# Holding the request of the fifth q and k until V of batch 1 has landed, in an attention and maxout-MLP kernel

## The chip, the cores and the metric

One core of a Trainium2 chip. The metric is device time in microseconds (us), the median of several executions. "Span" is the time from the first to the last instruction in the profile; the device time is 1.7 to 1.8 us more. Every execution reports the mean clock that TensorE was granted (1.000 is full), but only one of each set leaves a trace, so a trace always belongs to one execution with its own time. A run that is over 1.5% above the fastest of its kernel counts as slow; ratios leave such runs out, medians here keep them. A "hole" is a stretch in which TensorE stands idle, and the "flight" of a transfer is its time from request to landing.

## The reference

```python
# q, k, v: (8 batches, 8 heads, 576, 64)
attn = softmax(mask(q @ k.T / sqrt(64)))      # causal by blocks of 64
x = (attn @ v) as (4608 tokens, 512)
out = maximum(x @ w1, x @ w2) @ w_out         # w1, w2: (512, 1024), w_out: (1024, 512)
```

## The kernel before

The kernel runs attention for pairs of heads and fills TensorE's gaps with matmuls of the MLP. The 16 loads of q and of k ("groups" 0 to 15, two per batch) come through three buffers. A group's way is: transfer as float32, a Pool cast to bf16, TensorE transposes, copies, score matmuls.

```python
    def load_qk(g, queues, gated=False):
        ...
            raws[nm, g] = t = raw.tile([P, 2, RPP * D], FP32, name=f"{nm}raw")
            if gated:
                nc.gpsimd.memset(t[:, 0, :1], 0.0)     # one column: the transfer waits for Pool's turn
            queue.dma_start(out=t[:], in_=...)
```

A "gated" load can be requested only when Pool has come to its memset (the fifth q's starts at 38.41 us in the trace, the request follows at 38.55). Around the change, in program order (cuts marked):

```python
    load_qk(3, (SP, SP), gated=True)         # fourth q and k
    for c in range(NCH):
        load_v(1, c)                         # V of batch 1: five chunks, from Pool's DMA queue
    ...
    cast("q", 3, ((pool, 0, RPP),))
    cast("k", 3, ((pool, 0, RPP),))
    ...
    transposes("q", 3, (dve, act))()
    pool_work(4)                             # requests the fifth q and k (group 4)
    fill(n // 3)
    transposes("k", 3, (dve, act))()
    pad_keys(6)
    pad_keys(7)
    pool_work(5)                             # requests group 5, casts group 4
    ...
    for g in range(GPB + 1, NG):             # first turn, g = 3:
        ...
            av_with(p - LAG, lo)             # matmuls that read V of batch 1
            ...
            copy_out = t_pair(p)             # transposes of the fifth q
```

The whole kernel:

The softmax here doesn't subtract the row's maximum and nothing guards it: scores larger than these inputs give would overflow.

## Time and profile before

| | before |
|---|---|
| median of the first three runs | 259.31 us (259.14 to 260.01) |
| the run whose trace was read | 260.0 us, span 258.2 us |
| TensorE busy | 247.4 us, 96% |
| hole of TensorE before the fifth q's transposes, in that trace | 1.61 us |
| fifth q, request to landing | 38.55 to 46.06 us |
| last chunk of V of batch 1 lands | 44.87 us |

The lines are in the prediction. "PE" is TensorE, and an arrow in brackets names what ended an idle stretch.

### The profile page before, as it was taken

To read this page: it belongs to the slowest core of one execution; us is meant where nothing else is said; L and a number is where in the kernel's file an instruction comes from. 1 tells how busy PE (TensorE), PEld (TensorE's weight loads), DVE (VectorE), ACT (ScalarE), POOL (GpSimd) and SP (SyncE) were. 2 spreads that over 40 slices of the span, in tenths; PEclk is the share of its full clock that TensorE was granted. 3 is DMA by queue.
4 is the path that set the end of the run, shared out by engine and by line. 5 is a ranking of instruction groups with operands and counts; after the bars stand their busy time and mean duration, and the time that the engine had idled before them with its cause. 6 is when DMAs were issued, how large, how long until landed. Compare 5 with 4: busy or idle time off the path is not lost.

```text
span 258.2 us, 7195 instructions
## 1 busy us (share of the span) xinstructions
PE 247.4 (96%) x2983; PEld 139.1 (54%) x2983; DVE 136.1 (53%) x299; ACT 143.2 (55%) x200; POOL 110.4 (43%) x274
## 2 busy tenths in 40 slices
PE   7598899799999999999999999999999999999995
PEld 2346678646555555555555554546464655444444
DVE  4967986556584428451845184518550853443200
ACT  2798854476574857586757665766576431000111
POOL 1987950584637263726382638163813010000000
PEclk9999999999999999999999999999999999999999
DMA  6999999499569995998599949985977122202122
GB/s 244 316 206 307 217 251 246 156 102 253 129 162 257 144 188 135 245 154 225 114 244 143 186 145 224 168 196 141 91 109 110 44 56 80 83 0 81 43 104 99
DMA packets 71265, 41.30 MB, mean 160 GB/s; under 512 B 53568, under 2 KB 58048, under 8 KB 71232
## 3 DMA queue, kind: packets, MB, share of 16 engines
q1 hardware_dynamic: 28544, 31.27, 43.4%
q0 software_dynamic: 42272, 8.92, 39.9%
q10 hardware_dynamic: 416, 0.66, 0.7%
q8 instruction: 23, 0.38, 0.6%
q14 instruction: 10, 0.08, 0.1%
HBM read 34.60 MB, written 9.44 MB: 171 GB/s over the span
## 4 chain that ended last, share of the span: by engine, by line
PE 84%; DMA 8%; POOL 3%; ACT 2%; issue 1%; DVE 0%; SPq 0%; POOLq 0%; ACTq 0%
PE ps_y L257 36%; PE ps_h L215 22%; PE ps_o L479 10%; PE ps_s L371 8%; DMA qraw<-in_q_dram 5%; DMA kraw<-in_k_dram 3%; PE ps_qT L352 2%; PE ps_kT L352 2%; PE ps_w L341 1%; ACT aT L395 1%; PE ps_y L272 1%; PE ps_M L238 1%; POOL kn L132 1%; PE ps_s L389 1%; ACT qT L360 1%
## 5 line engine op out<-in xcount | busy, mean ns | idle before, releaser
L395 ACT ACTIVATE aT<-ps_s 128x1024 bf16<-128x1024 f32 (+2 forms) x100 | 95.8, 996 | 25.8 <-PE ps_s L371 24.2
L257 PE MATMUL ps_y<-wo_sb,g 128*128 128x512 bf16 x280 | 69.8, 379 | 0.0
L215 PE MATMUL ps_h<-xT,d_sb 128*128 128x512 bf16 (+3 forms) x320 | 69.2, 358 | 0.3 <-DVE d_sb L162 0.3
L220 DVE TENSOR_SCALAR g<-ps_h 128x512 bf16<-128x512 f32 (+3 forms) x80 | 50.7, 636 | 30.6 <-PE ps_h L215 28.8
L400 POOL MEMSET aT<- 64x128 bf16 x124 | 22.4, 200 | 81.8 <-ACT aT L395 81.2
L485 DVE RECIPROCAL rec<-ps_o 128x4 f32<-128x4 f32 (+1 forms) x64 | 12.1, 188 | 62.5 <-PE ps_o L479 61.7
L215 PEld LDWEIGHTS <-d_sb 128*128 128x128 bf16 x320 | 29.0, 98 | 29.1 <-issue 2.7
L479 PEld LDWEIGHTS <-aT 128*128 128x128 bf16 x960 | 37.2, 98 | 13.5 <-issue 0.8
L262 ACT COPY y<-ps_y 128x512 f32<-128x512 f32 x31 | 18.2, 587 | 44.5 <-PE ps_y L257 36.1
L257 PEld LDWEIGHTS <-g 128*128 128x128 bf16 x280 | 25.8, 98 | 29.8 <-issue 2.0
L479 PE MATMUL ps_o<-vv,aT 128*128 128x65 bf16 x960 | 39.8, 194 | 0.0
L257 PE MATMUL ps_y<-m_sb,xT 128*128 128x512 bf16 x140 | 38.2, 380 | 0.0
L136 POOL DMA_DIRECT2D vv<-in_v_dram x40 | 33.7, 848 | 1.6 <-issue 1.2
L371 PE MATMUL ps_s<-qT,kT 64*128 64x64 bf16 (+6 forms) x344 | 31.2, 280 | 1.6 <-ACT kT L360 0.7
L486 DVE TENSOR_TENSOR xp<-ps_o,rec 128x256 bf16<-128x256 f32 (+1 forms) x64 | 31.4, 491 | 2.2
L360 ACT COPY qT<-ps_qT 128x576 bf16<-128x576 bf16 (+1 forms) x17 | 10.3, 614 | 19.9 <-PE ps_qT L352 19.9
L132 POOL CAST qn<-qraw 128x1152 bf16<-128x1152 f32 (+1 forms) x16 | 16.9, 1058 | 9.1 <-DMA qraw<-in_q_dram 9.1
L257 PEld LDWEIGHTS <-xT 128*128 128x128 bf16 x140 | 12.2, 98 | 15.1 <-issue 3.5
L371 PEld LDWEIGHTS <-kT 64*128 64x128 bf16 x344 | 12.3, 94 | 11.0 <-issue 6.2
L132 POOL CAST kn<-kraw 128x1152 bf16<-128x1152 f32 (+1 forms) x15 | 17.1, 1140 | 1.4 <-DMA kraw<-in_k_dram 1.4
L360 ACT COPY kT<-ps_kT 128x576 bf16<-128x576 bf16 x15 | 9.6, 639 | 14.4 <-PE ps_kT L352 14.4
L207 POOL COPY g<-g 128x512 bf16<-128x512 bf16 x8 | 4.9, 614 | 20.7 <-DVE g L220 20.3
(58 smaller groups left out, 161.8 us busy)
## 6 DMA issues: line engine op xcount, KB each, us to landing
qraw<-in_q_dram SPq DMA_DIRECT2D x16, 576.0 KB, 5.0
out_dram<-y SPq DMA_DIRECT2D x35, 256.0 KB, 3.7
kraw<-in_k_dram SPq DMA_DIRECT2D x15, 576.0 KB, 5.8
vv<-in_v_dram POOLq DMA_DIRECT2D x32, 128.0 KB, 5.7
w1raw<-in_moe_w_dram POOLq DMA_DIRECT2D x4, 512.0 KB, 8.1
xT<-in_moe_w_dram POOLq DMA_DIRECT2D x4, 256.0 KB, 8.6
wo_sb<-in_moe_w_out_dram POOLq DMA_DIRECT2D x2, 512.0 KB, 10.0
kraw<-in_k_dram ACTq DMA_DIRECT2D x1, 576.0 KB, 5.6
```

The source lines that it names most:

```text
L132: copy(out=n[:, j0:j1], in_=t[:, j0:j1])
L136: nc.gpsimd.dma_start(out=vv_r[b % NV][P - rows:, c, :, :D], in_=v[b, :, c * P:c * P + rows, :].rearrange("h p d -> p h d"),)
L215: nc.tensor.matmul(pt[:, :w], d_sb[:, c, f * P:(f + 1) * P], xT[:, c, t0:t0 + w], start=(c == 0), stop=(c == NDM - 1),)
L220: nc.vector.tensor_scalar_max(g[:, f, m:m + w], pt[:, :w], 0.0)
L257: nc.tensor.matmul(py[:], lhs, rhs, start=(n == 0), stop=(n == len(terms) - 1),)
L262: (dve if i < 2 else act)(out=y[:], in_=py[:])
L360: (copy or copies[i])(out=t[:, p0 * RPP:p1 * RPP].rearrange("q (p j) -> q p j", j=RPP), in_=pts[i][:, :, p0:p1].rearrange("q j p -> q p j"),)
L371: nc.tensor.matmul(ps[:, hh, col:col + w], kT[r, k0:k0 + P], qT[r, q0:q0 + w], start=True, stop=True,)
L395: nc.scalar.activation(out=aT_r[p % NA][:, :, a0:a0 + w], in_=ps[:, :, :w], func=AF.Exp, scale=scale,)
L400: (eng or nc.gpsimd).memset(aT_r[p % NA][BLK:, :, a0:a0 + BLK], 0.0)
L479: nc.tensor.matmul(po[:, gi, hh, :], a[:, hh, a0:a0 + P], vv[:, c, h0 + 2 * hh, :], start=(mm == 0), stop=(mm == n_mm - 1),)
L486: nc.vector.tensor_mul(xp[:, :, ts[0]:ts[0] + n, p % 2].rearrange("q s t d -> q t s d"), po[:, :, :, :D], rec[:, :n].to_broadcast([P, n, 2 ...
```

## The change

V's small packets and the loads of q and k share the DMA engines from 38.5 us on: from there to 46 us the trace has 1911 packets (0.24 MB) in V's queue and 773 (1.69 MB) in that of q and k. The fifth q flew 7.51 us, against 4.0 to 5.1 us for the q loads requested after 50 us. The intent is to let V finish first, and to send q and k afterwards over free engines. To make Pool wait for V, the memset of one column is replaced by a copy that reads one element per chunk of V.

```diff
-    def load_qk(g, queues, gated=False):
+    def load_qk(g, queues, gated=False, behind=None):
...
             if gated:
                 nc.gpsimd.memset(t[:, 0, :1], 0.0)
+            if behind is not None:
+                nc.gpsimd.tensor_copy(out=t[:, 0, :NCH], in_=vv_r[behind][:, :, 0, 0])
             queue.dma_start(
...
         if s == 4:
-            load_qk(4, (SP, SP), gated=True)
+            load_qk(4, (SP, SP), behind=1)
```

## The prediction

> **What bounds the kernel now.** I read the page's sums first, then the chain of waits in order of time, then the timelines of TensorE and Pool around the place that the diff touches, and last the DMA view in narrow windows.
>
> ```profile
> PE 247.4 (96%) x2983; PEld 139.1 (54%) x2983; DVE 136.1 (53%) x299; ACT 143.2 (55%) x200; POOL 110.4 (43%) x274
> ...
> PE 84%; DMA 8%; POOL 3%; ACT 2%; issue 1%; DVE 0%; SPq 0%; POOLq 0%; ACTq 0%
> ```
>
> The reader is to see that TensorE is busy 96% of a span of 258.2 us, and that 84% of the chain that ends last is TensorE work. The rest of the chain lies almost wholly before 47.4 us; this is its part that holds the changed request (start, length, what):
>
> ```profile
> 28.34 8.94 DMA kraw<-in_k_dram
> 37.27 0.05 issue
> 37.33 1.15 POOL kn L132
> ...
> 38.55 7.51 DMA qraw<-in_q_dram
> 46.06 0.02 issue
> ...
> 46.18 1.16 POOL qn L132
> 47.34 0.05 issue
> 47.38 0.44 PE ps_qT L352 x18
> ```
>
> The transfer issued at 38.55 is the fifth q (batch 2, the one that the change holds back). So the changed request is itself on the path: issue, 7.51 us to landing, Pool's cast, TensorE's transposes. From 47.38 the chain is TensorE to the end. A table of stretches agrees: from 48 to 80 us TensorE is busy all 32.00 us, so a shift at 47.4 is carried to the end nearly one for one. TensorE's own timeline shows what the transfer costs today:
>
> ```profile
> 44.88 0.89 PE L479 MATMUL ps_o<-vv,aT 128*128 128x65 bf16 x24
> 47.38 0.44 PE L352 MATMUL ps_qT<-ident,qn 64*128 64x64 bf16 x18 [1.61 <-POOL qn L132]
> ```
>
> One hole of 1.61 us, from 45.77 to 47.38, ended by the cast of the fifth q. That is all that any improvement here can win, 0.6% of the time. The first of these lines is the user of V of batch 1. No hole stands before it: the last two chunks of V land at 44.35 and 44.87 in the trace, and the matmuls that wait for them start at 45.15 and 45.43, so V is 0.8 and 0.55 us early. V landing sooner buys TensorE nothing.
>
> Pool, which gates both requests:
>
> ```profile
> 38.41 0.10 POOL L119 MEMSET qraw<- 128x1 f32 x1
> 38.45 0.11 POOL L119 MEMSET kraw<- 128x1 f32 x1
> 41.69 0.53 POOL L378 COPY kz<-kT 128x128 bf16<-128x128 bf16 x2 [3.13 <-DVE kT L360]
> 42.16 0.10 POOL L119 MEMSET qraw<- 128x1 f32 x1
> 42.19 0.10 POOL L119 MEMSET kraw<- 128x1 f32 x1
> 46.18 1.15 POOL L132 CAST qn<-qraw 128x1152 bf16<-128x1152 f32 x1 [3.89 <-DMA qraw<-in_q_dram]
> ```
>
> Last, the DMA queues from 39.80 to 40.64 us and from 40.64 to 42.42 us (q0 carries V, q1 carries q and k):
>
> ```profile
> q0 software_dynamic: 211, 0.03, 260.1%
> q1 hardware_dynamic: 22, 0.05, 45.1%
> ```
>
> ```profile
> q1 hardware_dynamic: 147, 0.33, 83.3%
> q0 software_dynamic: 192, 0.02, 65.9%
> q8 instruction: 1, 0.02, 6.3%
> ```
>
> Of V's 4608 packets only a tail is left when the fifth q begins to move: 4129 packets went between 36 and 39.8 us. The tail sits on few of the 16 DMA engines: an engine alone starts one V packet every 13 ns, so 211 packets in 0.84 us are about three engines' work, 192 in the next 1.78 us less than two. One engine is last. The instruction fetch of 16 KB (q8) starts at 40.645 and takes 1.79 us; V's last 74 data packets start at 42.42, as it ends, and are through at 43.57. I read this as one engine that the fetch blocks in the middle of its V packets.
>
> [...] V from Pool's queue and q from SP's share the windows above. [...]
>
> **The change part by part.** Removed: two Pool memsets of one column, 0.10 us each. Added in their place: two Pool copies of 128x5 elements out of V of batch 1; an estimate of 0.1 to 0.2 us each, between that memset and the 0.27 us of the 128x128 copies. Nothing else moves: instruction by instruction the two built programs agree on all engines but for these two rows. The first copy waits for all five chunks of V.
>
> So the issue at 38.55 moves to the landing of V, plus copy and issue. When does V land without q beside it?
> - Upper end: as now, 44.87.
> - Lower end: the 13 engines that are on time end V at about 39.8. The two middle stragglers send their last V packet at 42.1 today; without q between, I put them at 41.7 (estimate), landing 42.1.
> - The last engine has its third chunk through at 40.31, 0.28 us later than the even pace of 0.85 us per chunk from 38.33 gives, so q has taken it only about 22 packets. At 40.645 it would have 74 - 22 = 52 packets left. The fetch comes at the same moment (TensorE's instructions up to there are the same). The other 22 fetches of this trace took 0.88 to 1.63 us, mostly about 1.1. 40.65 + 1.1 + 52 x 0.013 = 42.4 for the last packet; landing follows 0.4 to 1.3 us later in this trace. I choose 43.2.
>
> Issue of the fifth q: 43.2 + 0.2 = 43.4 instead of 38.55, that is 4.85 us later. Its flight gets shorter: nothing of V is left, all engines start even. Loads of q after 66 us take 4.0 to 5.05 us, mostly 4.0 to 4.4; I take 4.2 instead of 7.51, a gain of 3.3. Landing 47.6 instead of 46.06. Cast and hand-over stay 1.32 us (46.06 to 47.38). Transposes at 48.9 instead of 47.38: the hole grows from 1.6 to about 3.1 us. Sum: + 4.85 - 3.3 = + 1.5 us on the path.
>
> Off the path: the fifth k lands about 1.5 us after q, as now, and its transposes come 3.8 us after q's, with some 2.3 us of slack now. The key padding copies (41.69) slip to about 43.6; their reader runs after the transposes. The sixth q and k are requested near 44.5 instead of 42.28 and land by 53; they are transposed after 58 us. The masks wait behind Pool's casts and are read after 57 us. None binds.
>
> **The rivals.** First, V lands early and the sequenced transfers win: V at 41.7, q landing at 41.9 + 4.1 = 46.0. Then the hole is as it was, the time 259.2; with V at 41.3, 258.8. For it: 90% of V is through by 39.8 and 22 packets is a small stretch. Against it: the instruction fetch sits on an engine with V left, and that q's presence did not cause it. Second, V lands no earlier than 44.9 (the fetch takes its 1.8 us anyway): q lands at 45.1 + 4.2 = 49.3, + 3.2 us, 262.5. Third, the clock: [...] Fourth, the growth is absorbed by later holes: there are hardly any, 3.1 us in all after 80 us, most near the end.
>
> **Range and chances.** 259.31 + 1.4 = 260.7 (a tenth taken off for what later holes absorb). The first rival gives 259.0 to 259.3, the second 262.5; run to run the kernel spreads 0.9 us. Eight in ten: 259.3 to 262.4. Two per cent is 5.2 us. Faster by that is impossible, since the hole holds 1.6 us; slower would need V at 47 us, or the second and third rivals together with bad luck: 0.03. Faster 0.01, same 0.96.
>
> **What would show it.** In the changed kernel: the copy that reads V ends close to 43.3 (a step right if between 42 and 44); the fifth q is issued right after and takes 4 to 4.5 us; one hole of TensorE before the q transposes, of about 3.1 us, ended by Pool's cast; no hole at the matmuls on V; TensorE full from there on. I am wrong if V lands before 42, if the flight of q stays above 5 us, if the granted clock falls after the hole, or if a new hole opens at the k transposes or the sixth q.

## The result, and the profile after

| | before | changed |
|---|---|---|
| median | 259.22 us (6 runs, 258.30 to 260.01) | 262.58 us (6 runs, 261.49 to 263.33) |
| the run with the trace | 260.0 us | 263.33 us |
| its span, its granted clock | 258.2 us, 1.000 | 261.6 us, 0.993 |

The ratio is 1.0128 (95% interval 1.0094 to 1.0162). Ratios here are the mean time of one kernel's fast runs over that of the other's in the same rounds, so not quite the ratio of the medians. The change costs over 3 us where 1.4 was forecast, and the time lies just outside the range of 259.3 to 262.4. On which side of that edge it fell was partly chance: the same program in a later set (below) took 262.02. Both traces happen to be those of the slowest run of their set.

The page of the changed kernel, first the busy sum, then the granted clock in 40 slices of the span, in tenths (a 9 is 90% or more):

```profile
PE 249.9 (96%) x2983; PEld 140.3 (54%) x2983; DVE 136.0 (52%) x299; ACT 143.1 (55%) x200; POOL 110.2 (42%) x274
...
PEclk9999999899999999999999999999999999999999
```

TensorE runs the same 2983 matmuls but is busy 2.5 us longer, and one slice near 50 us has less than full clock. Of the 2.5 us, 0.7 lie before 38 us, ahead of the change; the rest must be slower work, since a longer wait alone would leave the busy time as it was. The chain of waits of the changed kernel in order of time (start, length, what):

```profile
31.34 12.18 DMA vv<-in_v_dram
...
43.75 0.19 POOL qraw L121
...
43.96 3.77 DMA qraw<-in_q_dram
...
47.85 1.15 POOL qn L134
49.01 0.05 issue
49.05 0.43 PE ps_qT L354 x18
```

V's landing at 43.51 is now on the path, ahead of q. The flight of q has halved, 7.51 to 3.77 us, but it starts 5.41 us later. TensorE's timeline at the same place:

```profile
45.02 0.89 PE L481 MATMUL ps_o<-vv,aT 128*128 128x65 bf16 x24
49.05 0.43 PE L354 MATMUL ps_qT<-ident,qn 64*128 64x64 bf16 x18 [3.14 <-POOL qn L134]
...
49.89 2.63 PE L240 MATMUL ps_M<-wo_sb,bT_sb 128*128 128x256 bf16 x12
```

In the kernel before, the same twelve matmuls of 256 columns read:

```profile
48.22 1.49 PE L238 MATMUL ps_M<-wo_sb,bT_sb 128*128 128x256 bf16 x12
```

So there are two things: the hole is 3.14 us in place of 1.61, and after it the same matmuls take 2.63 us in place of 1.49. Cut at the granted clock's own edges, the changed kernel shows why (columns: stretch, its length, busy time and instructions of TensorE, its weight loads, VectorE, ScalarE and Pool, then granted clock, DMA share, GB/s):

```profile
46.63:50.04 3.41, 0.99 (x30) 0.68 (x31) 0.62 (x2) 0.48 (x1) 1.80 (x2) 1.00 1.05 408
50.04:53.45 3.41, 3.41 (x22) 2.52 (x21) 1.20 (x5) 2.38 (x4) 1.65 (x7) 0.50 0.48 176
```

In the stretch of 3.41 us that holds most of the hole TensorE works only 0.99 us; in the next one its clock is 0.50. The half clock starts 44.373 us after the trace's first clock record, which is 13 times 3.413, and the record at full clock behind it lasts 208.213 us, 61 times 3.413; in the kernel before the one at full clock lasts 256.0 us, 75 times 3.413. So in each of these two traces the edges lie on a fixed grid; it lies elsewhere in each (edges at 46.63 us here, at 45.05 in the kernel before). From the first score matmul at full width after the q transposes to the k transposes, the chain takes 5.05 us (49.55 to 54.60) where it took 3.39 (47.88 to 51.27) before: 1.66 us more for the same work. The kernel before, at its own edges:

```profile
45.05:48.46 3.41, 1.79 (x55) 1.35 (x52) 1.71 (x5) 0.57 (x2) 1.90 (x2) 1.00 0.79 297
48.46:51.87 3.41, 3.41 (x76) 3.07 (x75) 2.04 (x7) 2.37 (x5) 1.65 (x7) 1.00 0.05 16
```

Its hole leaves TensorE 1.79 us of work in the stretch, and the clock stays full. Between the two traces the sum closes: 1.53 us more hole and 1.66 us of half clock are 3.19 of the 3.33 us between 260.0 and 263.33.

That leaves a riddle. Three of the changed kernel's six runs have a clock of 0.999, so by estimate no such stretch (3.41 us at 0.50 in a span of 261.6 us takes the mean to 0.993, as in the traced run), and still take 261.49 to 262.35 us: over 2 us more than the median before, where the two holes differ by 1.53.

### The profile page after: what moved, and what is told of

It reads as the page before. It is cut to its first block, busy times and chain, and to the rows that moved or that the text cites.

```text
span 261.6 us, 7197 instructions
## 1 busy us (share of the span) xinstructions
PE 249.9 (96%) x2983; PEld 140.3 (54%) x2983; DVE 136.0 (52%) x299; ACT 143.1 (55%) x200; POOL 110.2 (42%) x274
## 4 chain that ended last, share of the span: by engine, by line
PE 82%; DMA 10%; POOL 4%; ACT 1%; issue 1%; POOLq 0%; ACTq 0%
PE ps_y L259 36%; PE ps_h L217 22%; PE ps_o L481 10%; PE ps_s L373 7%; DMA vv<-in_v_dram 7%; DMA qraw<-in_q_dram 3%; PE ps_qT L354 2%; PE ps_kT L354 2%; POOL vv L138 2%; PE ps_M L240 2%; PE ps_y L274 1%; ACT aT L397 1%; PE ps_w L343 1%; PE ps_s L391 1%; POOL qn L134 1%
## 5 line engine op out<-in xcount | busy, mean ns | idle before, releaser
L362 DVE COPY qT<-ps_qT 128x576 bf16<-128x576 bf16 (+1 forms) x17 | 12.1, 712 | 3.2 <-PE ps_qT L354 2.9
## 6 DMA issues: line engine op xcount, KB each, us to landing
out_dram<-y SPq DMA_DIRECT2D x35, 256.0 KB, 3.6
xT<-in_moe_w_dram POOLq DMA_DIRECT2D x4, 256.0 KB, 8.6
```

Source lines behind the costliest of these rows:

```text
L362: (copy or copies[i])(out=t[:, p0 * RPP:p1 * RPP].rearrange("q (p j) -> q p j", j=RPP), in_=pts[i][:, :, p0:p1].rearrange("q j p -> q p j"),)
```

## The experiments

Ten kernels in three sets, each timed in rounds with the kernel before. All gave correct results.

**The kernel before, again.** No edit. The theory is that the trace read for the prediction had an unusually long hole, since its run was the slowest.

> The kernel before, run again unchanged, for a second trace. Theory A (the hole of 1.61 us belongs to the profiled run of 260.0 us, the slowest of six; in a run of the median, 259.2, it is about 0.8 us shorter): the time stays 258.3 to 260.0 and this trace's hole before the q transposes is 1.61 minus about (260.0 - its own time). Rival (the hole is fixed and the spread comes from elsewhere): the hole is 1.6 us whatever the time. No run has its clock below 0.999.

Measured: 258.95 us median (258.23 to 259.15); the traced run took 258.9. Its timeline at the place of the 1.61 us hole:

```profile
46.30 0.44 PE L352 MATMUL ps_qT<-ident,qn 64*128 64x64 bf16 x18 [0.47 <-POOL qn L132]
```

The hole is 0.47 us: 1.15 us shorter in a run 1.1 us faster. It goes with the flight of q: 38.54 to 44.98, 6.44 us in place of 7.51. Theory A holds. (The clock was 0.998 in three runs, where nothing below 0.999 was expected. They left no trace; the trace of the early request below, also 0.998, has half clock in its last 0.8 us only.) The hole in the kernel before varies from run to run, and 1.61 us was near the upper end, since no run of this kernel took over 260.04.

**The changed kernel with the hole partly filled.** Matmuls on zeros run where TensorE would wait.

```diff
+            if p == 2 * (GPB + 1):
+                warm_up(8)
             copy_out = t_pair(p)
```

> The changed kernel with 8 matmuls on zeros (about 0.216 us each, 1.7 us in all) issued where TensorE would stand idle before the q transposes; the transposes can start no earlier. Theory (of the excess, up to 1.7 us in a throttled run is half clock after the hole): every run has a clock of 0.998 or more and the median falls from 262.6 to 261.6. Rival (the clock record is a by-product): the median stays at 262.5 or rises.

Measured: 261.49 us median, ratio 1.0086 (1.0063 to 1.0109). Five of six runs had full clock and took 260.46 to 261.63; the sixth had a clock of 0.993 and took 264.5 (counted as slow, and not in the ratio). In the trace (261.44 us) 1.36 us of hole remain beside the 8 x 0.214 us of filler, so the wait was 3.07 us in all, as long as in the changed kernel, and the clock stayed full. The median is as expected; "every run" was wrong: 1.7 us of filler did not suffice in one run of six, which left no trace to say why.

**Waiting for one chunk of V only.** The copy stays, and what it waits for is there at 38.6 to 39.1 us.

```diff
-nc.gpsimd.tensor_copy(out=t[:, 0, :NCH], in_=vv_r[behind][:, :, 0, 0])
+nc.gpsimd.tensor_copy(out=t[:, 0, :1], in_=vv_r[behind][:, :1, 0, 0])
```

> The copies read and wait for the first of the five chunks of V only. It landed at 39.1 us in the changed kernel, so the request comes near 39.5 instead of 43.96. Theory (the cost is the later request, the more the later): hole and time within 0.5 us of the kernel before, 259.0 to 259.8, clock full. Rival (the read of V or the copy itself costs, whatever it waits for): 261 or more.

Measured: 258.61 us median, ratio 0.9982 (0.9962 to 1.0001). The request came at 38.83, q flew 5.14 us and landed at 43.97, and the trace has no hole there at all: the chain of waits runs through TensorE alone.

```profile
45.40 0.72 PE ps_o L481 x24
46.13 0.37 PE ps_qT L354 x18
```

The request came earlier than expected (38.83, not 39.5), and the median lies below the expected 259.0. So the copy and its reading of V cost nothing that can be seen; the hour of the request does.

**Only k waits for V.** q is requested as before. Pool itself is held until V has landed.

```diff
+            if behind is not None and nm == "q":
+                nc.gpsimd.memset(t[:, 0, :1], 0.0)
-            if behind is not None:
+            if behind is not None and nm == "k":
                 nc.gpsimd.tensor_copy(out=t[:, 0, :NCH], in_=vv_r[behind][:, :, 0, 0])
```

> The fifth q is requested at once as in the kernel before; only the fifth k waits for V, and so does Pool. Theory (the path goes through q alone, k has over 2 us of slack): no slower than the kernel before, 258.4 to 259.4; if k's packets also slow q, the flight of q drops below 7.5 us and the time by up to 1 us. Rival (holding Pool or k until V has landed costs by itself, for instance through the sixth q and k): 260.5 or more.

Measured: 258.96 us median, ratio 0.9997 (0.9968 to 1.0025). In the trace (259.7 us) k was requested at 44.99, 5.97 us later than in the trace read for the prediction, and the sixth q at 45.50 in place of 42.28, with no new hole. Pool's wait, the later k and the later sixth group are free. The flight of q stayed at 7.25 us, so in this trace the fifth k was not what slowed it, and the hoped-for gain did not come. The damage goes through the request of q alone.

**The changed kernel, again.** No edit.

> The changed kernel, run again unchanged, for a second trace and more pairs of time and clock. Theory (hole, and in some runs half clock for one window of 3.41 us): the runs fall into two groups, those with a clock of 0.998 or more at 261.4 to 262.4 and those near 0.992 some 1.2 to 1.7 us later; this trace's hole is 2.6 to 3.3 us. Rival (time does not go by the clock): the groups overlap.

Measured: 262.02 us median (260.19 to 264.59), ratio 1.0105 (1.0077 to 1.0132). The median of the five fast runs alone is 261.72. The trace fell on the slowest run (264.59 us, clock 0.987, counted as slow), so nothing is rested on it: its hole is 3.52 us, above the expected 2.6 to 3.3, and its half clock lasts two stretches. TensorE worked 0.82 us in the stretch before them and 2.49 us in the first of them. Together with the first set there are eleven fast runs of this program. Six with a clock of 0.999 or more take 260.19 to 262.35, mean 261.39 us; five with 0.991 to 0.993 take 262.33 to 263.33, mean 262.81. The groups touch rather than part, which was not expected, because the hole varies within each; their means differ by 1.42 us.

**The changed kernel with the hole filled by 12 matmuls.** The edit is that of the 8, with 12.

> As the kernel with 8 matmuls on zeros, with 12 (about 2.6 us), so that nearly all of the hole is filled. Theory: no run has half clock, all lie at 261.0 to 261.8, and the lead over the unchanged changed kernel in the same rounds is 0.6 to 1.2 us in the mean. Rival (filling costs as much as it saves): the mean is that of the changed kernel.

Measured: 261.12 us median (four runs, 260.92 to 261.67, all at 0.999 or more), ratio 1.0090 (1.0077 to 1.0103). No half clock, as expected. The lead over the unchanged program's fast runs of the same rounds is 261.60 - 261.21 = 0.39 us in the mean, less than expected: those rounds left out its slowest run, and in this trace q landed as early as 46.71, so that the filler ended after the cast and cost some 0.6 us itself. The filler removes the slow clock, not the wait: with 8 or 12 matmuls one run of ten has half clock, without them six of twelve.

**Waiting for three chunks of V.** The copy's slice is `[:, :3, 0, 0]`.

> The copies wait for the first three chunks of V. They landed by 42.1 in the changed kernel, so the request comes near 42.4. Theory (hole goes with the hour of the request): the fifth q lands near 46.3 after a flight of 3.8 to 4.3 us, the hole is 1.6 to 2.0 us and the time 259.9 to 260.6, between the one-chunk kernel and the changed one. Rival (only the last chunk matters, or any wait costs the same): below 259.3 or above 261.3.

Measured: 259.67 us median (258.92 to 262.44), ratio 1.0055 (1.0016 to 1.0094), between one chunk and five as expected, but the median a little under the stated range. In the trace (258.92 us, the fastest run) the third chunk was there at 40.86 rather than 42.1: request at 41.19, flight 3.80, hole 0.69 us. Two of the six runs had a clock of 0.993 and took 261.89 and 262.44. The hole in those isn't known, since they left no trace. An estimate: by the rule found below (258.4 us plus the hole) and with 1.4 to 1.7 us for half clock, it was 1.8 to 2.6 us.

**The opposite: an earlier request.** The fifth q and k are requested straight after the loads of V.

```diff
     for c in range(NCH):
         load_v(1, c)
+    load_qk(4, (SP, SP), gated=True)
...
         if s == 4:
-            load_qk(4, (SP, SP), gated=True)
+            pass
```

> The opposite of the change: the fifth q and k are requested as soon as Pool has issued the loads of V of batch 1, near 32 us instead of 38.55. Theory (the path is the landing of this q, V has slack): q lands before 43, no hole before its transposes, 258.2 to 258.7 unless V now lands after 45.1 and a new hole opens at the matmuls that read it. Rival (the DMA engines are the bound there, so whatever goes first delays V and the fourth q and k by as much): 259 or more, with a hole at the V matmuls or at the transposes of the fourth q.

Measured: 260.20 us median, ratio 1.0049 (1.0035 to 1.0063): slower, as the rival said. q landed at 39.23 and its hole is gone, but V's last chunk landed at 48.16 and TensorE now waits for V:

```profile
44.62 0.25 PE L479 MATMUL ps_o<-vv,aT 128*128 128x65 bf16 x3 [0.23 <-DMA vv<-in_v_dram]
...
46.26 0.37 PE L479 MATMUL ps_o<-vv,aT 128*128 128x65 bf16 x7 [0.67 <-DMA vv<-in_v_dram]
47.72 0.82 PE L479 MATMUL ps_o<-vv,aT 128*128 128x65 bf16 x15 [1.09 <-DMA vv<-in_v_dram]
```

Three holes of 1.99 us in sum in place of one. (The trace is that of the slowest run, 261.1 us. A fourth wait, for the chunk that landed at 48.16, is hidden in the 0.82 us of the last line; counted from start to start of the matmuls the four waits are 2.7 us.) At the two ends, this request and that of the changed kernel, one of q and V gains and the other loses; the kernel before is near the best of the request times tried. That no other order of requests does better is not shown.

**One chunk, again, and two chunks.** One chunk was the only kernel below the kernel before.

> The kernel that waits for one chunk of V, again, because it was the only one below the kernel before (258.61 against 258.92, the interval just touching 1). If the small gain is real (q meets less of V and flies some 1 us shorter for a delay of 0.3 us): 258.3 to 258.8 and a ratio below 1. If it was luck: a ratio of 0.999 to 1.001, and a hole of 0.3 to 0.8 us in the trace.

> The copies wait for two chunks of V; they landed between 39.6 and 41.0 in the traces so far. With time = 258.4 + hole (worked out from the traces so far at full clock), a request near 40.0 to 41.2 and a flight of 3.9 to 4.8 us give a hole of 0.2 to 0.9 us: 258.6 to 259.3, between one chunk and three. Rival (the loss comes in a step at the last chunks): the same as one chunk.

Measured: one chunk 258.93 us, ratio 0.9995 (0.9982 to 1.0008), hole 0.90 us in its trace (259.19), a little over the 0.8 expected; two chunks 258.76 us, ratio 0.9991 (0.9979 to 1.0003), hole 0.60 us. With two chunks the request came at 41.46, later than expected, and q flew 3.69 us, shorter than expected; the two misses cancel in the hole. The gain of one chunk was luck, or too small for five rounds; neither is shown to beat the kernel before. The loss doesn't come in a step: one and two chunks give ratios of 0.9995 and 0.9991 in the third set, three and five give 1.0055 and 1.0105 in the second.

**All traces together.** For those at full clock whose wait is seen:

| trace | its time | hole | time - hole |
|---|---|---|---|
| before, first | 260.0 | 1.61 | 258.4 |
| before, again | 258.9 | 0.47 | 258.4 |
| k alone waits | 259.7 | 1.38 | 258.3 |
| one chunk, again | 259.2 | 0.90 | 258.3 |
| two chunks | 259.1 | 0.60 | 258.5 |
| three chunks | 258.9 | 0.69 | 258.2 |
| changed, 8 fillers | 261.4 | 3.07 with the filler | 258.4 |

The time is 258.4 us plus the hole, within 0.2. Left out are traces with half clock and three more: the first one with one chunk has no hole and took 258.65 (its matmuls on V start at 45.24, not 44.88); with 12 fillers the wait is overfilled; with the early request TensorE waits for V. This solves the riddle. The rounds' median of the kernel before, about 259.0, means a hole near 0.6 us (worked out by this rule, not traced); the mean of the changed kernel's runs at full clock, 261.39, means one near 3.0. The hole grows by 2.4 us, not by 1.5, and half clock adds 1.42 us in five of eleven runs, 0.65 in the mean: 3.05 us together, against 2.7 and 3.3 us from the two ratios.

## Why the prediction was wrong

Its mechanism held, and nearly every number on the path came out:

| step | predicted | trace of the changed kernel |
|---|---|---|
| last V packet (the records don't name its engine) | 42.4 | 42.75 |
| V landed | 43.2 | 43.51 |
| fifth q requested | 43.4 | 43.96 |
| flight of q | 4.2 | 3.77 |
| q landed | 47.6 | 47.73 |
| transposes begin | 48.9 | 49.05 |
| hole | about 3.1 | 3.14 |
| slack of k, of group 5, of the masks | none binds | no new hole |

That the hole came out within 0.04 us is in part luck: the request came 0.56 us later than predicted, and the flight was 0.43 us shorter. The path through q alone was right (k alone held back: 0.9997), and so was V's slack.

**The first failed term: the hole of the kernel before.** The prediction wrote "One hole of 1.61 us" and then "the hole grows from 1.6 to about 3.1 us. Sum: + 4.85 - 3.3 = + 1.5 us", and added this to the median of 259.31. But the 1.61 us was that of a run of 260.0 us. The result list on the same page said so. By the rule above a run of 259.31 us has a hole near 0.9 us, so from there the growth is 2.2 us, not 1.5; from the later rounds' 259.0 it is 2.4 us. An increment measured against one run was added to another run's time; this mis-sized the sum by about 0.7 us. Put on its own run, 260.0 + 1.5 = 261.5 would have met the runs at full clock.

**The second failed term: the clock, rival three.** It got no weight in the 260.7. In the traced run a hole of 3.14 us was followed by a stretch of 3.41 us at a clock of 0.50. What the traces show beside the hole is little work of TensorE within one stretch of the grid: after 0.99 us of work in 3.41 came half clock, after 1.79 (the kernel before) and 2.05 (8 fillers) full clock. Whether the clock goes by that work, and where between 0.99 and 1.79 us it would turn, no run shows; in the slow trace of the changed kernel 2.49 us of work in a stretch at half clock was followed by a second one at half clock. The price was 1.66 us in the trace, 1.42 between the groups' means. It falls in five of eleven fast runs.

With both terms sized so, 258.4 + 3.1 + 0.65 gives 262.15 us, against a mean of 262.04 us over the eleven fast runs. This is a sum after the fact, from the same runs, and no test of its own.

**What stays open.** Why the kernel before lands q anywhere from 44.98 to 46.06. The prediction read the late V as one DMA engine held up by an instruction fetch, about 1.1 us. Over the eleven traces other than that of the early request, this fetch starts between 39.4 and 40.7 us and takes 1.5 to 1.9 us, with q in flight or without (the prediction took 1.1); the last V packet starts 1.7 to 3.1 us after it. With the changed kernel's own fetch the prediction's sum gives 40.58 + 1.51 + 52 x 0.013 = 42.8, against the traced 42.75. That is in accord with the reading. So is a pattern over the five traces in which q was requested between 38.4 and 39.2 us: with the fetch at 39.6 us (two traces) q lands at 43.97 and 44.98, at 40.22 it lands at 45.25, and at 40.5 to 40.7 (two) at 45.72 and 46.06; in all five q lands 2.0 to 2.7 us after the last V packet starts. But the records don't name the engine of a packet and no experiment moved a fetch, so it is argued, not shown, and what moves the fetch is open.

## What to carry to other kernels

A trace is one run: before an increment is added to a median, look at which run the trace belongs to, and take a second trace when a wait on the path depends on DMA traffic (here the same hole was 1.61 us in one trace and 0.47 in the next). Holding a transfer back to clear the way for another pays only if its own flight shortens by more than the delay; here 5.4 us of delay bought at most 3.7 us, while the transfer that was protected had slack already. When a change lengthens an idle stretch of TensorE to two or three microseconds (here 3.14 in a trace, 1.8 to 2.6 by estimate in two runs), count a possible half-clock stretch into the price with a real weight (here 1.42 to 1.66 us, in five of eleven fast runs).
